# W1's load begun behind the filter's half swaps, the last group's evacuations reordered on ScalarE and VectorE, and 12 identity matmuls where 28 were

## The chip, the cores and the metric

The kernel runs on one core of a Trainium2 chip. The metric is the device time of one execution in microseconds (us). On one core a run is called slow if it lies over 1.5% above the fastest of its kernel. Each run also carries the mean clock that TensorE was granted, 1.000 being full speed.

Engines in the profile: PE is TensorE (PEld its weight loads), DVE is VectorE, ACT is ScalarE, POOL is GpSimd, SP is SyncE, whose sequencer (SPq) issues nearly all DMAs here.

## The reference, cut to what matters

```python
x = A_q                                              # 2048 tokens x 512 channels, bf16
x = x + A(layernorm(x), A_k, A_v, A_shift_k, A_ssm_k, A_ssm_D)
x = x + B(layernorm(x), B_w1, B_b1, B_w2, B_b2)
# both once more
# A(q, ...): kv = shift(k) * v;  y = irfft(rfft(kv) * rfft(ssm_k)) + kv * ssm_D;  q * y
# B(x, ...): gelu(layernorm(x) @ w1 + b1) @ w2 + b2
```

`y` in A depends on `k`, `v` and the filter only, so the kernel computes the long convolution once. It is a two-stage transform by matrices: filter (K), input (U), product (T), and back (V, Y). Then come eight MLP groups (four token groups, twice), of two matmul stages each, which need W1 and W2.

## The kernel before

The program is a list of named pieces, and one string fixes the order on every engine. The letter behind the dot is the engine (P, D, A, G, S for PE, DVE, ACT, POOL and SP); digits are buffer slots. Each engine works through its pieces strictly in this order, waiting where data is missing (DVE waits 1.48 us for a swap ahead of T00, for instance, with its later pieces behind it).

```python
ORDER = """ ...
... lM.S ... sw10.S ... U0T0.P0 pb0.G
w1.S K215e.A ... sw01.S ... sw00.S kv2.P12 ... U2T0.S1 ... U1T0.S2 ... U1T1.S ... U2T1.S ... sw11.S X11e.A0 ...
U3T0.S0 ... U3T1.S ... X30.P0 ... V32f.A gs0.D V33f.A TP22.S Y02e.A TP03.P3
V33r.A ga1.D TP03e.A TP31.S gs1.D V32r.A Y03.P1 TP30.S Y03e.A TP13.P0 gl0.D TP23.P3 TP13e.A TP33.P2 lx1.S TP23e.A
Y10.P0 gl1.D gp0.G ... gb0.D gp1.G gb1.D LT0.P0 TP33e.D LT1.P1 LT0e.A gb2.D TP21.S LT1e.A
m10x0.P3 pa10.D m10x1.P2 ge0x0.A pa11.D LT2.P0 lx2.S m10y0.P1 w2.S LT2e.D ge0x1.A pb1.G ...
"""
# w1: W1, 1.4 MB, one load from HBM
w1 = load("w1", W1t[:], B_w1.rearrange("(ct p) f -> p ct f", p=P), 3600)
# sw00 .. sw11: the filter's spectrum with its halves swapped, SBUF to SBUF, 1 MB each
def swap(it, off=off):
    for a in range(2):
        queue(it).dma_start(at(KSW + off, [[1, 16 * 256]], a, 64, 2), at(off, [[1, 16 * 256]], 1 - a, 64, 2))
# U1T0 .. U3T1: DMA transposes that feed the second transform stage X10 .. X33
nc.sync.dma_start_transpose(ztv(xown or it, [NA, P])[:, 16 * h:16 * h + 16, :],
                            ztv(own, [NA * P])[:, 2048 * h:2048 * h + 2048])
# T00 ..: DVE multiplies a spectrum by the filter and by the swapped filter (L528)
eng.tensor_tensor(spec(), x2, spec(), ALU.mult)
# ... cut ...
IDLE = (28, 0, 0)
for t in range(IDLE[h]):                              # L683, ahead of LT0's transposes
    nc.tensor.matmul(o.bitcast(F32)[:, 0, 0:64], IDt[:], IDt[:, 0:64], start=True, stop=True)
```

Names used below: T00 is the first spectral multiply, needing swap `sw00`. U3T0 and U3T1 are the last pair of transposes, X30 is the matmul group that needs U3T0. TP03 and TP13 are PE transposes of the output side, with TP03e the evacuation of the first. Y03 needs TP03e. V32r and V33r are the remainders of two evacuations, which TP13 needs. LT2e evacuates PE transposes that end late. pa11 is the second half of group 1's layer norm statistics. m110 is the first full gelu block of group 1.

Of the kernel before, what the change touches and what calls it, by code (L numbers as in the profile page):

```python
# [20 lines left out]
K200.P1 K2T0e.D K206.P2 K200e.A lk2.S K3T1.P3 K206e.D kv0.P01 K3T1e.A lk1.S K207.P2 kvm01.D K2T1.P3 K207e.A kvm00.D  # L21
K2T1e.A K3T0.P2 lM.S U0S0.P0 K3T0e.D U0S1.P1 U0S0e.A4 K204.P3 U0S1e.D K210.P2 K204e.A K211.P0 K210e.A K211e.D K212.P1
K213.P3 K212e.A U0S3.P2 K213e.D U0S2.P0 U0S3e.A K205.P1 U0S2e.D sw10.S K216.P3 K215.P2 K216e.A K205e.D U0T0.P0 pb0.G
w1.S K215e.A K202.P3 U0T0e.D5 sw01.S K203.P1 K202e.A K201.P2 K203e.D X00.P0 K201e.A U0T1.P3 X00e.A0 sw00.S kv2.P12
U0T1e.D kv1.P03 kvm20.D kvm21.D kvm11.D U2S0.P1 U2S1.P2 U2S0e.A6 kvm10.D U2S1e.A U2S2.P1 U2S2e.D U2S3.P0 U1S0.P3
U2S3e.A U1S3.P2 U1S0e.D0 U1S1.P1 U1S3e.A U2T0.S1 U1S2.P0 U1S1e.D K217.P3 U1S2e.A X01.P2 T00.D K217e.A K214.P1 U1T0.S2
X03.P0 K214e.A X02.P3 X01e.D1 X02e.A2 V00.P1 T01.D X03e.A0 kv3.P23 U1T1.S T02.D V00e.A3 T03.D X20.P0 pc00.G U2T1.S
V01.P1 kvm31.D X20e.A1 V01e.A kvm30.D X10.P0 X10e.A2 X11.P1 T20.D pc01.G U3S0.P2 sw11.S X11e.A0 U3S3.P3 T10.D X13.P0
U3S0e.A4 U3S2.P1 X13e.D1 U3S2e.A V10.P2 U3S3e.A T11.D X12.P0 X21.P1 V10e.A5 V03.P3 X12e.D2 X21e.A0 U3S1.P2 T13.D
V02.P0 U3S1e.A V20.P1 T12.D V03e.A U3T0.S0 V13.P2 V20e.D6 V02e.A V12.P3 V13e.A T21.D U3T1.S X23.P0 V12e.A X22.P1  # L30
X23e.D1 V11.P2 X22e.A2 V21.P3 TP00.S2 T23.D V11e.A X30.P0 V21e.A X31.P1 T22.D V23.P2 X31e.A0 V22.P3 V23e.D TP01.S
X30e.A1 X32.P1 T31.D V22e.A X33.P2 TP10.S1 Y00.P0 X33e.A2 T30.D V31.P3 X32e.A0 TP02.S T33.D Y01.P2 Y00e.A V30.P1
Y01e.A TP12.S T32.D V33.P0 V30e.A4 ga0.D V32.P2 TP11.S V31e.A Y02.P1 ho.G V32f.A gs0.D V33f.A TP22.S Y02e.A TP03.P3
V33r.A ga1.D TP03e.A TP31.S gs1.D V32r.A Y03.P1 TP30.S Y03e.A TP13.P0 gl0.D TP23.P3 TP13e.A TP33.P2 lx1.S TP23e.A
Y10.P0 gl1.D gp0.G TP20.S Y10e.A Y11.P3 Y11e.A gb0.D gp1.G gb1.D LT0.P0 TP33e.D LT1.P1 LT0e.A gb2.D TP21.S LT1e.A
m10x0.P3 pa10.D m10x1.P2 ge0x0.A pa11.D LT2.P0 lx2.S m10y0.P1 w2.S LT2e.D ge0x1.A pb1.G m10y1.P3 ge0y0.A TP32.S
m10z0.P0 pc10.D pc11.D ge0y1.A pd10.D m10z1.P2 ge0z0.A pd11.D m10z2.P1 ge0z1.A pe10.D Y21.P3 lx3.S ge0z2.A Y20.P0
pe11.D Y20e.A m200.P2 Y21e.A pa21.D pf1.G pg11.A pa20.D pg10.A lt11.S m201.P1 pa30.D pb2.G lt10.S pc20.A ad00.D pa31.D
pc21.A pa40.D m110.P0 pb3.G pc31.A pd21.D m111.P3 pd20.D ge10.A m112.P2 ge11.A pe21.D m113.P0 ge12.A pe20.D m114.P3
# [70 lines left out]
class _Plan:  # L110
# [7 lines left out]
    def add(self, name, cost, deps, fn, take=(), free=(), after=(), dma=0, tr=0):  # L118
        it = dict(name=name, cost=cost, deps=[d for d in deps if d is not None], fn=fn, take=list(take), slot={},
                  free=list(free), after=list(after), dma=dma, tr=tr)  # L120
        self.items.append(it)
        return it
# [15 lines left out]
def kernel(ctx: ExitStack, tc: tile.TileContext, A_q, A_k, A_v, A_shift_k, A_ssm_k, A_ssm_D,  # L138
# [186 lines left out]
    def load(name, dst, src, ns, deps=(), after=()):  # L325
        return add(name, {"S": 400, **QUEUE.get(name, {})}, deps, lambda it: queue(it).dma_start(dst, src), dma=ns, after=after)
# [227 lines left out]
    w1 = load("w1", W1t[:], B_w1.rearrange("(ct p) f -> p ct f", p=P), 3600)  # L554
# [5 lines left out]
    w2 = add("w2", {"S": 1300}, Vall[:8], w2load, dma=3900)  # L560
# [93 lines left out]
    POOLED = ("pc00", "pc01")  # L654
    CH = ((0, 1), (1, 2), (2, 4))
    GLC = ((0, 2), (2, 4))
    IDLE = (28, 0, 0)

    def gate_first(ln):
        gs = []  # L660
# [16 lines left out]
        for h, (a, b) in enumerate(CH):  # L677
# [3 lines left out]
            def mms(o, h=h, a=a, b=b):  # L681
                for t in range(IDLE[h]):
                    nc.tensor.matmul(o.bitcast(F32)[:, 0, 0:64], IDt[:], IDt[:, 0:64], start=True, stop=True)  # L683
                for i in range(a, b):
                    for ct in range(CT):
                        nc.tensor.transpose(o[:, CT * (i - a) + ct, :], lna0[:, i, ct * P:(ct + 1) * P], IDt[:])
# [124 lines left out]
```

## Time and profile before

| | before |
|---|---|
| time, six runs | 250.77 us median (249.75 to 253.33) |
| profiled run | span 249.2 us, mean clock 0.992 |
| T00's wait on the swap | 1.48 us |
| U3T0: issued, needed by X30 | 66.49, 71.53 us |
| 28 identity matmuls | 0.98 us |
| m110 starts | 111.12 us, without a wait |

Page of the kernel before, its strips of 40 slices of 6.2 us each (busy tenths; the granted clock in tenths; the DMA engines' busy tenths).

```profile
PE   7999999877999689999999999999999999999994
PEclk9999999999999799999999999999999999999999
DMA  6999999999399899440401240400310250030132
```

PE is full from slice 16 on, which is the MLP. What comes earlier decides when that stretch begins. The one 7 of the clock strip is a short stretch at half speed.

Waits view of the kernel before (engine, output, line, who ended the wait; us in total, times, longest), then its timeline (start us, duration us, engine, line, operation; in brackets the idle time ahead and who ended it).

```profile
DVE low L528 <- DMA low<-low: 1.5, 1, 1.5
```

```profile
48.72 1.21 DVE L359 CAST ZT_77<-p_89 128x1024 bf16<-128x1024 f32 x1
51.41 1.23 DVE L528 TENSOR_TENSOR low<-xb_84,low 128x2048 bf16<-128x2048 bf16 x1 [1.48 <-DMA low<-low]
...
66.49 4.44 SPq L477 DMA_TRANSPOSE ZT_77<-ZT_81  x2
71.53 0.61 PE L517 MATMUL p_88<-ZT_77,Wt 128*128 128x128 bf16 x8
...
81.23 0.62 PE L583 MATMUL p_91<-IDt,ZT_81 128*128 128x128 bf16 x8 [0.41 <-ACT ZT_81 L544]
83.33 0.41 PE L597 MATMUL p_89<-ZT_79,GPt 128*64 128x512 bf16 x2 [1.49 <-ACT ZT_79 L335]
84.04 0.62 PE L583 MATMUL p_88<-IDt,ZT_81 128*128 128x128 bf16 x8 [0.30 <-ACT ZT_81 L544]
88.47 0.98 PE L683 MATMUL p_88<-IDt 128*128 128x64 bf16 x28 [0.32 <-ACT high L335]
...
111.12 1.89 PE L738 MATMUL p_88<-low,W1t 128*128 128x512 bf16 x8
```

DVE starts T00 1.48 us late, for a swap still on its way. Further down, X30 (71.53 us) begins with no wait shown, 5.0 us after U3T0 was issued. TP03 (81.23) and TP13 (84.04) start 2.81 us apart. Windows view (stretch; length, busy time of PE, PEld, DVE, ACT and POOL with counts, granted clock, DMA share, GB/s):

```profile
44.00:46.00 2.00, 1.30 (x11) 1.02 (x12) 2.00 (x2) 1.33 (x2) 0.47 (x1) 1.00 1.02 411
46.00:48.00 2.00, 2.00 (x19) 1.57 (x17) 1.78 (x3) 1.69 (x3) 0.00 (x0) 1.00 1.02 427
...
64.00:66.00 2.00, 2.00 (x35) 1.91 (x33) 2.00 (x3) 1.92 (x3) 0.00 (x0) 1.00 0.00 0
...
84.00:88.00 4.00, 3.96 (x32) 2.59 (x32) 3.29 (x15) 3.02 (x4) 0.73 (x2) 0.57 0.93 200
```

DMA is full at 44 to 48 us, when the swaps are awaited, and empty at 64 to 66 us. The clock of 0.57 over 84 to 88 us is the half-speed stretch, some 3.4 us of it (us by us from 84: 0.77, 0.50, 0.50, 0.52, then 1.00).

### The profile page before, as it was taken

The page shows a single profiled execution, that of the slowest core. Times are in us where ns is not written, and L with a number is a line of the kernel's source. Part 1 is how long each engine was busy: PE and PEld are TensorE (multiplying, and loading weights), DVE is VectorE, ACT ScalarE, POOL GpSimd, SP SyncE. Part 2 cuts the span into 40 slices and gives each one's busy share as a digit, 9 for nine tenths or more (in the row PEclk, how much of TensorE's full clock was granted, in tenths as well). Part 3 has the DMA queues.
Part 4 walks back from the last instruction along what each step waited for, and adds up shares of the span by engine and source line. Part 5 has one row for each costly group of instructions (what it writes and reads, how often), then busy time and mean ns, then how long its engine had stood idle before and what let it go on. Part 6 is the DMA issues. An engine that isn't in the chain of part 4 may idle for free.

```text
span 249.2 us, 4803 instructions
## 1 busy us (share of the span) xinstructions
PE 234.9 (94%) x1910; PEld 146.5 (59%) x1919; DVE 170.4 (68%) x337; ACT 150.0 (60%) x217; POOL 50.6 (20%) x78
## 2 busy tenths in 40 slices
PE   7999999877999689999999999999999999999994
PEld 7888879676997579444444444444444444444443
DVE  2778697979999898999899967459749210110322
ACT  2598894778999869977738296172065463064000
POOL 4189970105001111230401121010110100000000
PEclk9999999999999799999999999999999999999999
DMA  6999999999399899440401240400310250030132
GB/s 228 269 420 161 241 393 293 360 184 235 115 189 187 171 224 256 108 84 1 86 3 37 49 84 3 84 0 1 72 15 0 45 123 3 0 84 0 45 73 54
DMA packets 55306, 31.02 MB, mean 125 GB/s; under 512 B 49810, under 2 KB 51956, under 8 KB 54260
## 3 DMA queue, kind: packets, MB, share of 16 engines
q1 hardware_dynamic: 54130, 30.38, 52.0%
q10 hardware_dynamic: 1074, 0.33, 0.6%
q8 instruction: 15, 0.25, 0.4%
q0 software_dynamic: 80, 0.00, 0.2%
q14 instruction: 7, 0.06, 0.1%
HBM read 12.36 MB, written 2.10 MB: 58 GB/s over the span
## 4 chain that ended last, share of the span: by engine, by line
PE 74%; DMA 9%; DVE 7%; ACT 6%; issue 2%; SPq 0%; DVEq 0%
PE p_90 L764 9%; PE p_91 L764 9%; PE p_88 L738 8%; PE p_89 L764 8%; PE p_91 L738 8%; PE p_90 L738 8%; PE p_89 L738 6%; DMA high<-in_A_k_dram 6%; PE p_88 L764 5%; DMA low<-in_A_ssm_k_dram 3%; ACT low L335 2%; ACT ZT_81 L544 1%; PE p_91 L536 1%; DVE low L528 1%; DVE high L469 1%
## 5 line engine op out<-in xcount | busy, mean ns | idle before, releaser
L738 PEld LDWEIGHTS <-W1t 128*128 128x128 bf16 (+1 forms) x440 | 40.2, 100 | 36.8 <-issue 0.6
L764 PEld LDWEIGHTS <-low 128*128 128x128 bf16 (+1 forms) x363 | 35.3, 98 | 41.2 <-issue 0.8
L749 ACT ACTIVATE low<-p_91,B_72 128x512 bf16<-128x512 f32 (+2 forms) x31 | 15.7, 581 | 17.1 <-PE p_90 L764 6.4
L749 ACT ACTIVATE low<-p_90,B_72 128x512 bf16<-128x512 f32 (+4 forms) x27 | 15.3, 633 | 17.5 <-PE p_89 L764 10.3
L749 ACT ACTIVATE low<-p_88,B_72 128x512 bf16<-128x512 f32 (+2 forms) x26 | 15.6, 658 | 14.0 <-PE p_89 L764 9.8
L764 PE MATMUL p_90<-low 128*128 128x512 bf16 (+3 forms) x107 | 23.4, 368 | 0.2
L738 PE MATMUL p_88<-low,W1t 128*128 128x512 bf16 (+2 forms) x104 | 22.9, 362 | 0.0
L764 PE MATMUL p_91<-low 128*128 128x512 bf16 (+1 forms) x95 | 22.0, 379 | 0.2
L738 PE MATMUL p_91<-low,W1t 128*128 128x512 bf16 (+2 forms) x124 | 21.7, 322 | 0.5 <-ACT low L335 0.5
L772 DVE TENSOR_TENSOR high<-p_91,high 128x1024 bf16<-128x1024 f32 (+1 forms) x5 | 5.6, 1115 | 24.1 <-PE p_91 L764 24.1
L738 PE MATMUL p_90<-low,W1t 128*128 128x512 bf16 (+4 forms) x108 | 21.8, 345 | 0.0
L764 PE MATMUL p_89<-low 128*128 128x512 bf16 (+3 forms) x99 | 21.0, 367 | 0.0
L738 PE MATMUL p_89<-low,W1t 128*128 128x512 bf16 (+4 forms) x104 | 17.8, 317 | 0.0
L536 PEld LDWEIGHTS <-low 128*128 128x128 bf16 x256 | 14.7, 98 | 3.0 <-DVE low L528 2.7
L749 ACT ACTIVATE low<-p_89,B_72 128x512 bf16<-128x512 f32 (+4 forms) x26 | 13.1, 577 | 1.3 <-PE p_89 L738 1.3
L287 ACT ACTIVATE high<-high,lnm_99,lrs_98 128x512 bf16<-128x512 bf16 x12 | 9.0, 840 | 7.2 <-POOL lnm_99 L276 7.2
L616 DVE TENSOR_TENSOR high<-high 128x1024 bf16<-128x1024 bf16 (+1 forms) x16 | 10.7, 668 | 2.8 <-ACT high L287 1.9
L764 PE MATMUL p_88<-low 128*128 128x512 bf16 (+1 forms) x53 | 12.3, 379 | 0.1
L772 DVE TENSOR_TENSOR high<-p_89,high 128x1024 bf16<-128x1024 f32 (+1 forms) x4 | 4.1, 1025 | 9.3 <-PE p_89 L764 9.3
L264 DVE BATCH_NORM_STATS2 lst_104<-high 128x6 f32<-128x512 bf16 x16 | 10.3, 683 | 0.3 <-DMA high<-in_A_q_dram 0.2
L264 DVE BATCH_NORM_STATS2 lst_96<-high 128x6 f32<-128x512 bf16 x16 | 10.2, 682 | 0.1
L274 POOL TENSOR_TENSOR lrs_98<-lrs_98,mhalf 128x4 f32<-128x4 f32 x4 | 4.0, 1007 | 30.4 <-DVE lnm_99 L271 30.4
(220 smaller groups left out, 442.8 us busy)
## 6 DMA issues: line engine op xcount, KB each, us to landing
low<-low SPq DMA_DIRECT2D x8, 512.0 KB, 11.0
low<-in_A_ssm_k_dram SPq DMA_DIRECT2D x4, 512.0 KB, 6.1
high<-in_A_v_dram SPq DMA_DIRECT2D x2, 1024.0 KB
high<-tabM SPq DMA_DIRECT2D x1, 2048.0 KB, 9.7
high<-in_A_q_dram SPq DMA_DIRECT2D x6, 256.0 KB, 5.4
W1t<-in_B_w_dram SPq DMA_DIRECT2D x1, 1376.0 KB, 10.7
low<-in_B_w_dram SPq DMA_DIRECT2D x1, 1280.0 KB, 8.8
Wt<-tabW SPq DMA_DIRECT2D x1, 1024.0 KB, 14.3
```

The costliest lines, as they stand in the source:

```text
L264: nc.vector.bn_stats(self.st[:, i, h, :], xg(g, i, i + 1, c0, c9)[:, 0, :])
L274: nc.gpsimd.tensor_tensor(self.rs[:, a:b], self.rs[:, a:b], mhalf[:, a:b], ALU.pow)
L287: nc.scalar.activation(dst[:, i, :], xs, AF.Identity, bias=bi, scale=sc)
L335: nc.scalar.activation(d, s, AF.Copy)
L469: nc.vector.tensor_tensor(us, k, us, ALU.mult)
L528: eng.tensor_tensor(spec(), x2, spec(), ALU.mult)
L536: nc.tensor.matmul(o[:, i, :], T[:, r, i, :], Mt[:, k0 + i, r, :], start=r == 0, stop=r == 1)
L616: nc.vector.tensor_tensor(tmp[:, a:b, c0:c9], ln[:, a:b, c0:c9], ys, ALU.mult)
L738: nc.tensor.matmul(o[0:m, ft - fts[0], :], W1t[:, ct, ft * P:ft * P + m], lnT[n % 3][:, a:b, ct, :], start=ct == 0, stop=ct == CT - 1)
L749: nc.scalar.activation(hT[n % 2][0:m, ft, a * P:b * P], psv(pe, dims)[0:m, ft - fts[0], :], AF.Gelu_apprx_tanh, bias=B1[0:m, ft:ft + 1])
L764: nc.tensor.matmul(o[:, i - a, 0:c9 - c0], hT[n % 2][0:m, ft, i * P:(i + 1) * P], W2t[0:m, ft, c0:c9], start=ft == 0, stop=ft == FT - 1)
L772: nc.vector.tensor_tensor(xs, psv(pe, [2, D])[:, 0:b - a, 0:c9 - c0], xs, ALU.add)
```

## The change

Its intent: keep W1's transfer out of the way of the swaps that T00 awaits; let Y03 start sooner by evacuating TP03 first; bring LT2's evacuation and gb2 forward on DVE; spend fewer identity matmuls. The diff, with unmoved words cut:

```diff
-w1.S K215e.A ... sw01.S ... sw00.S ... U2T0.S1 ... U1T0.S2 ... U1T1.S ... U2T1.S ... sw11.S X11e.A0
+K215e.A ... sw01.S ... sw00.S ... U2T0.S1 ... U1T0.S2 ... U1T1.S ... U2T1.S ... sw11.S w1.S X11e.A0
-TP03.P3 V33r.A ga1.D TP03e.A TP31.S gs1.D V32r.A Y03.P1
+TP03.P3 ga1.D TP03e.A V33r.A TP31.S gs1.D V32r.A Y03.P1
-LT0.P0 TP33e.D LT1.P1 LT0e.A gb2.D TP21.S LT1e.A
+LT0.P0 LT1.P1 LT0e.A gb2.D TP33e.D TP21.S LT1e.A
-m10x1.P2 ge0x0.A pa11.D LT2.P0 lx2.S m10y0.P1 w2.S LT2e.D ge0x1.A pb1.G
+m10x1.P2 ge0x0.A LT2.P0 lx2.S m10y0.P1 w2.S LT2e.D pa11.D ge0x1.A pb1.G
-    IDLE = (28, 0, 0)
+    IDLE = (12, 0, 0)
```

More of the change, by code (lines that the diff above doesn't have):

```diff
@@ L23 @@
 K213.P3 K212e.A U0S3.P2 K213e.D U0S2.P0 U0S3e.A K205.P1 U0S2e.D sw10.S K216.P3 K215.P2 K216e.A K205e.D U0T0.P0 pb0.G
-w1.S K215e.A K202.P3 U0T0e.D5 sw01.S K203.P1 K202e.A K201.P2 K203e.D X00.P0 K201e.A U0T1.P3 X00e.A0 sw00.S kv2.P12
-U0T1e.D kv1.P03 kvm20.D kvm21.D kvm11.D U2S0.P1 U2S1.P2 U2S0e.A6 kvm10.D U2S1e.A U2S2.P1 U2S2e.D U2S3.P0 U1S0.P3
-U2S3e.A U1S3.P2 U1S0e.D0 U1S1.P1 U1S3e.A U2T0.S1 U1S2.P0 U1S1e.D K217.P3 U1S2e.A X01.P2 T00.D K217e.A K214.P1 U1T0.S2
-X03.P0 K214e.A X02.P3 X01e.D1 X02e.A2 V00.P1 T01.D X03e.A0 kv3.P23 U1T1.S T02.D V00e.A3 T03.D X20.P0 pc00.G U2T1.S
-V01.P1 kvm31.D X20e.A1 V01e.A kvm30.D X10.P0 X10e.A2 X11.P1 T20.D pc01.G U3S0.P2 sw11.S X11e.A0 U3S3.P3 T10.D X13.P0
+K215e.A K202.P3 U0T0e.D5 sw01.S K203.P1 K202e.A K201.P2 K203e.D X00.P0 K201e.A U0T1.P3 X00e.A0 sw00.S kv2.P12 U0T1e.D
+kv1.P03 kvm20.D kvm21.D kvm11.D U2S0.P1 U2S1.P2 U2S0e.A6 kvm10.D U2S1e.A U2S2.P1 U2S2e.D U2S3.P0 U1S0.P3 U2S3e.A
+U1S3.P2 U1S0e.D0 U1S1.P1 U1S3e.A U2T0.S1 U1S2.P0 U1S1e.D K217.P3 U1S2e.A X01.P2 T00.D K217e.A K214.P1 U1T0.S2 X03.P0
+K214e.A X02.P3 X01e.D1 X02e.A2 V00.P1 T01.D X03e.A0 kv3.P23 U1T1.S T02.D V00e.A3 T03.D X20.P0 pc00.G U2T1.S V01.P1
+kvm31.D X20e.A1 V01e.A kvm30.D X10.P0 X10e.A2 X11.P1 T20.D pc01.G U3S0.P2 sw11.S w1.S X11e.A0 U3S3.P3 T10.D X13.P0
 U3S0e.A4 U3S2.P1 X13e.D1 U3S2e.A V10.P2 U3S3e.A T11.D X12.P0 X21.P1 V10e.A5 V03.P3 X12e.D2 X21e.A0 U3S1.P2 T13.D
@@ L33 @@
 Y01e.A TP12.S T32.D V33.P0 V30e.A4 ga0.D V32.P2 TP11.S V31e.A Y02.P1 ho.G V32f.A gs0.D V33f.A TP22.S Y02e.A TP03.P3
-V33r.A ga1.D TP03e.A TP31.S gs1.D V32r.A Y03.P1 TP30.S Y03e.A TP13.P0 gl0.D TP23.P3 TP13e.A TP33.P2 lx1.S TP23e.A
-Y10.P0 gl1.D gp0.G TP20.S Y10e.A Y11.P3 Y11e.A gb0.D gp1.G gb1.D LT0.P0 TP33e.D LT1.P1 LT0e.A gb2.D TP21.S LT1e.A
-m10x0.P3 pa10.D m10x1.P2 ge0x0.A pa11.D LT2.P0 lx2.S m10y0.P1 w2.S LT2e.D ge0x1.A pb1.G m10y1.P3 ge0y0.A TP32.S
+ga1.D TP03e.A V33r.A TP31.S gs1.D V32r.A Y03.P1 TP30.S Y03e.A TP13.P0 gl0.D TP23.P3 TP13e.A TP33.P2 lx1.S TP23e.A
+Y10.P0 gl1.D gp0.G TP20.S Y10e.A Y11.P3 Y11e.A gb0.D gp1.G gb1.D LT0.P0 LT1.P1 LT0e.A gb2.D TP33e.D TP21.S LT1e.A
+m10x0.P3 pa10.D m10x1.P2 ge0x0.A LT2.P0 lx2.S m10y0.P1 w2.S LT2e.D pa11.D ge0x1.A pb1.G m10y1.P3 ge0y0.A TP32.S
 m10z0.P0 pc10.D pc11.D ge0y1.A pd10.D m10z1.P2 ge0z0.A pd11.D m10z2.P1 ge0z1.A pe10.D Y21.P3 lx3.S ge0z2.A Y20.P0
```

## The prediction

> **What bounds the kernel.** From about 102 us to the end it is TensorE: in the windows view PE is busy 140.6 of 141.0 us from 104 to 245 us, with 1.73 us per eight-matmul block and no waits. The change touches nothing there. So it can only move the moment at which that stretch starts, set by the first 102 us. Before: DVE is busy nearly without a gap from 51.4 to 79.3 us (27 pieces, about 1.13 us apart, in the DVE timeline), then the last filter group passes ACT and PE (79 to 90 us).
>
> **Step 1, W1's load.** Its 1.4 MB are issued at 35.8 us, ahead of three of the half swaps. The DMA queues are full there (share about 1.0, 300 to 430 GB/s). The waits view shows one DVE wait on these swaps: 1.48 us before the first spectral multiply, 49.93 to 51.41 us. At about 330 GB/s W1 is worth some 4 us of DMA time (estimate), so the swap then lands before 49.9 us and the wait goes: -1.5 us. DVE is full behind it, so this carries to 79 us. The skew-in transposes behind (2.8 to 3.4 us each to issue) should be quicker too. W1 now goes out at 56 to 60 us, into an empty hole (64 to 66 us: 0 GB/s), and is needed only at 88 us. It may hold up the last pair of transposes (issued at 66.5 us, needed at 71.5): +0.3 us expected. [...]
>
> **Step 2, ScalarE.** The transpose's evacuation (0.92 us) now stands ahead of a remainder evacuation (0.70 us) that used to fill the 0.36 us in which its transpose finishes. Y03 starts about 0.7 us sooner, but its evacuation and the next transposes (which wait for both remainders) come 0.36 us later; the gate waits for that evacuation (84.47 to 84.51 us). Expected +0.3 us. PE ran at clock 0.50 from 84.4 to 87.9 us, after idling 1.49 us. [...] The idle time is shared out otherwise, not removed, so I expect this cold stretch still, or moved.
>
> **Step 3, identity matmuls.** 28 take 0.98 us on the chain, at 88.47 us, when their input's producer (DVE) is already done at 88.5. 16 fewer: -0.56 us.
>
> **Step 4, VectorE.** The second statistics of group 1 now stand behind the evacuation of LT2, whose transposes end only at 93.4 us. DVE idles about 1.2 us there, and group 1's gate starts some 2.2 us later than the shift allows. Before, its last transposed load was issued about 106.8 us, landing 3.2 us later at 110.0; its consumer on PE came at 111.28, so slack was about 1.3 us. Now PE would be there at 109.6 and the load at about 110.8: a new PE wait of about 1.2 us eats most of the gain.
>
> **Sum.** -1.5 +0.3 +0.3 -0.6 +1.2 = -0.3; if the last is smaller than I think, -1.7. I predict 249.9 us, between 248.4 and 251.3; faster over 2% 0.02, same 0.96, slower 0.02.
>
> **What would show it.** No DVE wait on the swap DMA; PE at the first full gelu block (111.28 us before) between 109.5 and 111.3, with a wait there on the transposed load; 12 identity matmuls taking 0.4 us; ACT idle about 0.4 us ahead of the moved evacuation; W1 landing before 72 us.
>
> **What would make it wrong.** The half clock vanishing (-1 us) or falling on the first gelu blocks (+1.7 us); W1 delaying the last transposes; slack at group 1 other than read.

That PE's idling brings the half-speed stretch was the estimate from this one trace, where the stretch follows 1.49 us of idle time. The clock's -1 and +1.7 us under what would make it wrong are estimates too: 1.7 is half of the stretch measured here (3.4 to 3.5 us); for -1 the record gives no source, and the runs counted below differ by 0.95 us between none and one stretch.

## The result

| | before | changed |
|---|---|---|
| median of all runs | 250.72 us (40 runs) | 254.82 us (20 runs, 253.12 to 257.61) |
| fast runs, ratio | | 1.0155, 95% interval 1.0132 to 1.0178 |
| profiled run | span 249.2 us, clock 0.992 | span 251.8 us, clock 0.993 |

A ratio is the mean time of one kernel's fast runs over that of the other's of the same rounds, so it is not quite the ratio of the medians. The change is slower by 1.55%, about 3.9 us, where 249.9 us was predicted, with 251.3 us as the upper end. It stays within 2%, the class that was given 0.96, but with the opposite sign: a small gain was forecast and a clear loss measured. That the class fits is due to its width, not to the account behind it.

Waits view of the changed kernel:

```profile
PE p_88 L517 <- DMA ZT_77<-ZT_81: 2.3, 1, 2.3
PE p_88 L738 <- DMA low<-high: 1.9, 1, 1.9
```

Its timeline:

```profile
49.73 1.21 DVE L528 TENSOR_TENSOR low<-xb_84,low 128x2048 bf16<-128x2048 bf16 x1
...
60.06 0.73 SPq L326 DMA_DIRECT2D W1t<-in_B_w_dram  x1
64.79 6.93 SPq L477 DMA_TRANSPOSE ZT_77<-ZT_81  x2
...
72.30 0.62 PE L517 MATMUL p_88<-ZT_77,Wt 128*128 128x128 bf16 x8 [2.30 <-DMA ZT_77<-ZT_81]
...
82.00 0.62 PE L583 MATMUL p_91<-IDt,ZT_81 128*128 128x128 bf16 x8 [0.41 <-ACT ZT_81 L544]
83.73 0.41 PE L597 MATMUL p_89<-ZT_79,GPt 128*64 128x512 bf16 x2 [1.11 <-ACT ZT_79 L335]
85.14 1.03 PE L583 MATMUL p_88<-IDt,ZT_81 128*128 128x128 bf16 x8 [1.00 <-ACT ZT_81 L544]
89.55 0.51 PE L683 MATMUL p_88<-IDt 128*128 128x64 bf16 x12 [0.69 <-ACT high L335]
...
113.77 0.59 PE L738 MATMUL p_88<-low,W1t 128*128 128x512 bf16 x2 [1.87 <-DMA low<-high]
```

Its windows:

```profile
44.00:46.00 2.00, 1.32 (x12) 1.04 (x12) 2.00 (x2) 1.46 (x2) 0.34 (x1) 1.00 0.07 29
46.00:48.00 2.00, 2.00 (x18) 1.57 (x17) 1.78 (x3) 1.69 (x3) 0.00 (x0) 1.00 0.00 0
...
64.00:66.00 2.00, 2.00 (x40) 2.00 (x38) 2.00 (x3) 2.00 (x3) 0.00 (x0) 1.00 1.01 380
...
72.00:74.00 2.00, 1.70 (x31) 1.71 (x32) 0.00 (x0) 0.55 (x1) 0.00 (x0) 1.00 1.27 285
```

And from the chain of waits that ended last, the two DMA pieces (start, length):

```profile
64.79 7.46 DMA ZT_77<-ZT_81
...
109.51 4.12 DMA low<-high
```

T00 now starts at 49.73 us instead of 51.41, as foretold. PE arrives at X30 at 70.00 us (72.30 less its wait), 1.53 us ahead of the kernel before, and then waits 2.30 us: U3T0, issued at 64.79 us while W1 keeps the DMA engines at 380 GB/s, takes 7.46 us to land. So X30 starts 0.77 us later than before (72.30 against 71.53), although PE was there 1.53 us sooner. The hole in the DMA traffic has moved from 64 us, where U3T0 was issued into it, to 44 us, where nothing uses it. TP03 and TP13 are 3.14 us apart instead of 2.81. At m110 PE waits another 1.87 us.

The two profiled runs have the same clock and differ by 2.6 us, the medians by 4.1. The clocks of the 21 runs of the change (the profiled one and 20 more, among them one slow run) explain most of the rest. One stretch of 3.4 us at half speed (3.42 us in both profiled runs, by windows of 1 us from 84 us on) lowers the mean clock of a 250 us run by 3.4 x 0.5 / 250 = 0.0068. Counted this way (the deficit of the mean clock over 0.0068, rounded), with the 44 runs of the kernel before that were taken alongside the experiments, so not in the same rounds:

| half-speed stretches in a run | before: runs, mean us | changed: runs, mean us |
|---|---|---|
| 0 | 24, 250.07 | 1, 253.35 |
| 1 | 20, 251.02 | 8, 253.58 |
| 2 | | 7, 255.10 |
| 3 or 4 | | 5, 256.36 |

With one stretch on both sides the change costs 253.58 - 251.02 = 2.56 us. The kernel before has 20/44 = 0.45 stretches a run, the changed one (8 + 14 + 12 + 4)/21 = 1.8. An estimate from these means: the mean of the changed kernel's 20 fast runs lies 1.0 us above its runs with one stretch, that of the kernel before 0.5 us below its own, so the additional stretches cost about 1.5 us. With the 2.56 us that makes 4.1, against 3.9 by the ratio and 4.1 by the medians.

### The profile page after: what moved, and what is told of

The parts are those of the page before. It is cut to its first block, busy times and chain, and to the rows that moved or that the text cites. A ratio compares the mean times of both kernels' runs of the same rounds, so it can differ in the third digit from the quotient of the medians.

```text
span 251.8 us, 4773 instructions
## 1 busy us (share of the span) xinstructions
PE 234.3 (93%) x1894; PEld 146.2 (58%) x1903; DVE 170.1 (68%) x337; ACT 149.8 (59%) x217; POOL 50.1 (20%) x78
## 4 chain that ended last, share of the span: by engine, by line
PE 61%; DMA 14%; DVE 12%; ACT 6%; issue 4%; POOL 1%; SPq 0%; DVEq 0%
PE p_91 L764 8%; PE p_91 L738 8%; PE p_88 L738 8%; PE p_90 L738 7%; PE p_90 L764 7%; PE p_89 L764 6%; DMA high<-in_A_k_dram 6%; PE p_89 L738 5%; PE p_88 L764 5%; DMA ZT_77<-ZT_81 3%; DMA low<-in_A_ssm_k_dram 3%; DVE low L528 2%; DMA low<-high 2%; ACT ZT_81 L544 2%; DVE high L469 1%
```

## The experiments

All were run in five rounds beside the kernel before, on the same chip within a group (e1 to e4, e5 to e8, e9 to e12, e13 and e14), and all gave correct results. In their profiles line numbers are one or two off, as the order string was wrapped anew, and buffer numbers are missing. The reading in us is the ratio less 1, times the 250.3 to 250.8 us of the kernel before in that group.

### e1 to e4: each part of the change alone

The theory was that W1's new place and VectorE's reorder make the loss; the rival, that W1's move is the gain predicted and all the loss lies in the reorders.

```diff
 e1: ORDER  - pb0.G w1.S K215e.A        + sw11.S w1.S X11e.A0
 e2: ORDER  - V33r.A ga1.D TP03e.A      + ga1.D TP03e.A V33r.A
 e3: ORDER  - TP33e.D ... gb2.D         + gb2.D TP33e.D
            - pa11.D ... LT2e.D         + LT2e.D pa11.D
 e4: IDLE   - (28, 0, 0)                + (12, 0, 0)
```

Expected of e1: 

> Only the move of W1's load, from ahead of three half swaps to behind the last one. Theory (W1's transfer sits in the DMA queues ahead of the last pair of transposes, and so gives back more than the swaps gain): DVE's 1.48 us wait on the swap is gone, PE waits some 2 to 2.5 us for the last pair of transposes near 72 us, net +0.8 to +1.5 us. Rival (the move of W1 is a gain of about 1 us, as predicted, and the loss lies in the reorders): -1 us.

Expected of e2: 

> Only ScalarE's reorder (the transpose's evacuation ahead of the first remainder). Theory: the next transposes wait for both remainders, so they and the gate come 0.3 to 0.4 us later: +0.3 to +0.6 us. Rival (the sooner Y03 helps the clock, or the chain): 0 to -0.5 us.

Expected of e3: 

> Only VectorE's two reorders. Theory: the second statistics of group 1 wait behind the evacuation of LT2, so group 1's transposed tile lands some 2 us later and PE waits at its first full gelu block: +1.2 to +2.2 us. Rival (there is slack enough): 0, and no such wait.

Expected of e4: 

> Only 12 identity matmuls in place of 28. Theory A: they are plain work on the chain: -0.4 to -0.6 us, and the granted clock of the runs is as before. Theory B: the 28 keep PE's clock up, and with 12 more runs fall to half clock for one more stretch of 3.4 us: +0.3 to +1.5 us, with clocks of 0.987 and lower in more of the runs.

(Theory B of e4 is a guess that no earlier run had shown; its 3.4 us is the stretch of the kernel before, 84.5 to 88 us.)

| | median us | ratio to before | 95% interval | us |
|---|---|---|---|---|
| e1, W1 alone | 251.77 | 1.0074 | 1.0043 to 1.0106 | +1.85 |
| e2, ScalarE alone | 250.61 | 1.0011 | 0.9979 to 1.0042 | +0.3 |
| e3, VectorE alone | 251.77 | 1.0059 | 1.0029 to 1.0089 | +1.5 |
| e4, 12 identity matmuls | 250.10 | 0.9994 | 0.9955 to 1.0033 | -0.15 |
| sum | | | | +3.5 |
| whole change | 254.82 | 1.0155 | 1.0132 to 1.0178 | +3.9 |

The parts nearly add up, and two of them make the loss. The rival about W1 falls: its move alone costs 1.85 us. That is more than the theory's upper end of 1.5; it brings half-speed stretches too, 1.3 a run by the count above against 0.45 before, and e13 below tests that. The timeline of e3 shows VectorE's part, here beside that of the kernel before. First before:

```profile
91.62 1.28 DVE L264 BATCH_NORM_STATS2 lst_104<-high 128x6 f32<-128x512 bf16 x2
...
93.52 0.69 DVE L337 COPY low<-p_88 128x1024 bf16<-128x1024 bf16 x1
94.73 1.38 DVE L289 TENSOR_SCALAR high<-high,lrs_106,lnm_107 128x512 bf16<-128x512 bf16 x4 [0.51 <-POOL lnm_107 L276]
```

Then e3:

```profile
92.69 0.69 DVE L336 COPY low<-p 128x1024 bf16<-128x1024 bf16 x1 [0.49 <-PE p L685]
93.29 1.28 DVE L263 BATCH_NORM_STATS2 lst<-high 128x6 f32<-128x512 bf16 x2
96.39 0.73 DVE L288 TENSOR_SCALAR high<-high,lrs,lnm 128x512 bf16<-128x512 bf16 x2 [1.33 <-POOL lnm L275]
...
111.32 2.97 PE L737 MATMUL p<-low,W1t 128*128 128x512 bf16 x13 [0.87 <-DMA low<-high]
```

Before, pa11 (91.62 us) filled the time until LT2's transposes were done, so the copy at 93.52 us hardly waited. In e3 DVE waits for PE first and does pa11 afterwards. The next step, which needs POOL's scale made from pa11, starts 1.66 us later (96.39 against 94.73) although PE runs ahead, and at m110 PE waits 0.87 us. Its time, +1.5 us, is more than this wait; the profiled run had no half-speed stretch, and what makes up the rest was not looked into.

The time of e2 is inconclusive: its interval holds both theories. Its trace is not. TP03 and TP13 are 3.15 us apart (80.99 and 84.14 us), against 2.81 before and 3.14 in the change. The reorder costs 0.34 us at this place, as predicted. e4's time is inconclusive as well; its 12 identity matmuls and those of the change save 0.47 us of PE time (0.51 against 0.98), and no clear gain can be told from that.

### e5, e6, e7: the same load elsewhere

```diff
 e5: ORDER  - pb0.G w1.S K215e.A        + sw00.S w1.S kv2.P12
 e6: ORDER  - pb0.G w1.S K215e.A        + U3T1.S w1.S X23.P0
 e7: ORDER  - pb0.G w1.S K215e.A        + sw11.S w1.G X11e.A0
```

Expected of e5: 

> Only the move of W1's load, but to just behind the third half swap, some 20 us sooner than in the change. Theory (what hurts is W1's 1.4 MB lying in the queues ahead of the last pair of transposes): W1 fills the hole that the changed kernel's trace shows from 44 to 48 us (0 to 29 GB/s), the DVE wait on the swap is gone, the last pair of transposes lands about 5 us after issue, PE does not wait for it: -0.8 to -1.6 us. Rival (moving W1 behind the swaps costs wherever it goes, as it delays other transposes): 0 to +1 us, with PE waits on the earlier pairs.

Expected of e6: 

> Only the move of W1's load, to behind the last pair of skew-in transposes (about 68 us). Theory: the pair lands about 5 us after issue again, so the wait near 72 us is gone, but W1 now lies ahead of the transposes of the output side, of which the first is needed by PE some 5 us later: PE waits there instead, 1 to 3 us; net 0 to +2 us. Rival (only the last pair was tight): -1 to -1.5 us.

Expected of e7: 

> W1's load moved as in the change, but issued by GpSimd[...]. Theory A (the transposes stand behind W1 in one queue, in order): beside another queue they get a share at once and land in 5 to 6 us, PE waits under 1 us: -1 to 0 us. Theory B (the bytes alone count, whichever queue they are in): the transposes take 7 us and more as in the change, PE waits about 2.3 us: +0.8 to +1.9 us.

| | ratio | 95% interval | us | U3T0's time on the queue | PE's new wait |
|---|---|---|---|---|---|
| before | 1 | | | 1.83 us | none |
| e5, behind the third swap | 0.9980 | 0.9948 to 1.0012 | -0.5 | 1.88 us | 1.22 us at X10, 1.17 us at X30 |
| e1, behind the last swap | 1.0074 | 1.0043 to 1.0106 | +1.85 | 4.05 us | 2.39 us at X30 |
| e6, behind the last pair | 1.0160 | 1.0122 to 1.0198 | +4.0 | 1.92 us | 3.27 us at Y00 |
| e7, as e1, issued by POOL | 1.0147 | 1.0114 to 1.0180 | +3.7 | 4.96 us | 3.33 us at X30 |

(The time on the queue is how long SP's sequencer is busy with issuing that one transpose.) T00 starts at 49.5 to 49.8 us in all four variants: every place behind the third swap frees DVE from the wait. What differs is which transposes follow W1. In e6 the pair is quick again and the next consumer, PE's Y00, waits instead. That loss is twice what was expected at most. Part of the losses of e6 and e7 is clock: they had 1.8 and 2.2 half-speed stretches a run. e6's profiled run, with one, took 252.52 us and its other five, with two, 254.5 to 255.2. e7 refutes the idea that the transposes only stand behind W1 in one ordered queue:

```profile
57.53 0.87 POOL L325 DMA_DIRECT2D W1t<-in_B_w_dram  x1
...
64.63 4.96 SPq L476 DMA_TRANSPOSE ZT<-ZT  x1
...
73.17 1.89 PE L516 MATMUL p<-ZT,Wt 128*128 128x128 bf16 x16 [3.33 <-DMA ZT<-ZT]
```

These lines are e7's timeline. W1 is issued by another engine, 2.6 us earlier than in e1, and takes 12.2 us to land instead of 8.8; the transposes get no better service beside it than behind it: U3T0 takes 4.96 us on SP's queue and 8.5 us to land, against 4.05 and 7.55 us in e1. So a load that another engine issued holds the transpose up as well. It fits theory B in direction, though the wait was 1 us above what B expected and the time, +3.7 us, twice its upper end. e7 is not the same load on another queue and nothing else: it went out ahead of sw11 (58.14 us), not behind it, and the profile page of e7 shows its 1.4 MB on q0, "software_dynamic", where e1 has them on q1, "hardware_dynamic". Which of these made the load itself slower was not tried.

e5's time is inconclusive: -0.5 us is less than the theory asked for, and the interval holds 0. Its trace shows that the rival is partly right:

```profile
57.44 1.07 PE L516 MATMUL p<-ZT,Wt 128*128 128x128 bf16 x16 [1.22 <-DMA ZT<-ZT]
...
71.79 1.07 PE L516 MATMUL p<-ZT,Wt 128*128 128x128 bf16 x16 [1.17 <-DMA ZT<-ZT]
```

W1 now lies ahead of the earlier pair of transposes, and PE waits 1.22 us at X10 (57.44 us). That delays the evacuations which U3T0 needs, so U3T0 is issued at 65.56 us, where e1 has 64.73. Its profiled run also shows 1.17 us of wait at X30, with no W1 left in the queues (it had landed 9.1 us after its issue at 40.7 us). In e11, with the same place for W1, X10 waited likewise (1.34 us), but X30 did not. So the landing of the last pair varies by about 1 us between runs (U3T0: 6.18 us in e5, 4.9 us at most in e11, where X30 starts at 70.36 us after an issue at 65.46), for a reason that stays open.

### e8: which of VectorE's two reorders

```diff
 e8: ORDER  - pa11.D ... LT2e.D         + LT2e.D pa11.D
```

Expected of e8: 

> Of VectorE's two reorders only the second: the second statistics of group 1 behind the evacuation of LT2. Theory (this one makes the loss): DVE idles 0.5 to 1.3 us before that evacuation, PE waits about 0.9 us for group 1's transposed tile: +0.9 to +1.6 us. Rival (the other reorder makes it, or both together): under +0.5 us.

Measured: 251.44 us, ratio 1.0038 (1.0008 to 1.0068), +0.95 us; DVE idles 1.8 us ahead of LT2's evacuation and PE waits 0.9 us at m110, as in e3. The idle time is above the 1.3 us expected at most, the time as expected. So this reorder alone loses, though only just clear of noise. The intervals of e3 and e8 overlap, so whether the other reorder adds anything is not settled.

### e9: half the load

```diff
+    w1r = B_w1.rearrange("(ct p) f -> p ct f", p=P)
-    w1 = load("w1", W1t[:], B_w1.rearrange("(ct p) f -> p ct f", p=P), 3600)
+    w1 = load("w1", W1t[:, 0:2, :], w1r[:, 0:2, :], 1800)
+    w1b = load("w1b", W1t[:, 2:4, :], w1r[:, 2:4, :], 1800)
 ORDER  - pb0.G w1.S K215e.A      + sw00.S w1.S      + sw11.S w1b.S
```

Expected of e9: 

> W1's load in two halves of 0.7 MB: one behind the third half swap, one where the change has the whole. So far: the last pair's first transpose took 7.5 us from issue to landing with all of W1 ahead of it, 6.2 us with none, and PE waited 2.3 and 1.2 us. Theory (the bytes ahead of it count): about 6.8 us, PE waits 1.5 to 2.0 us, time between the two: +0.3 to +1.2 us over the kernel before. Rival (a plain load of any size ahead costs the same, as a matter of order): 7.5 us and 2.3 us, +1.5 us.

Measured: 250.05 us, ratio 0.9971 (0.9942 to 0.9999), -0.7 us. This missed both expectations: PE had no wait at X30 and 0.23 us at X32. U3T0's time on the queue was 2.91 us, between the 1.9 us of no W1 and the 4.0 us of the whole. So the bytes count for the time on the queue. Half of them, issued at 59.92 us, were further through when U3T0 was issued at 64.64 us: the window of 64 to 66 us has 246 GB/s, against 398 in e1. That what is still in flight then decides, and not the bytes issued ahead, is a reading of these two windows and was not tested by itself. For PE's wait half a load can't be told from none: it was 0 here and 1.37 us in e14 with half, 1.17 us in e5 and 0 in e11 with none.

### e10, e12, e13: the change with one thing put back, and the clock

```diff
 e10: the change, IDLE  - (12, 0, 0)  + (28, 0, 0)
 e12: the change, ORDER - LT2e.D pa11.D  + pa11.D ... LT2e.D
 e13: the change, and ahead of X30's matmuls (shortened: the program picks X30 by a parameter):
+    for t in range(64):
+        nc.tensor.matmul(o[:, 0, 0:64], IDt[:], IDt[:, 0:64], start=True, stop=True)
```

Expected of e10: 

> The whole change, but with the 28 identity matmuls kept. Theory A (they are plain work): 0.4 to 0.6 us slower than the change, so +4.2 to +4.7 us over the kernel before, clocks spread as in the change (most at 0.987 and below). Theory B (the missing 16 cost clock): the same as the change or faster, +3 to +4 us, with more runs at 0.993 and 1.0.

Expected of e12: 

> The change with only the statistics of group 1 put back ahead of the evacuation of LT2. Theory (the parts add up): 1.0 to 1.9 us faster than the change, so +2.0 to +2.9 us over the kernel before; no PE wait at the first full gelu block. Rival (the late W1 delays this stage anyway): +3.5 us, wait still there.

Expected of e13: 

> The whole change, with 64 identity matmuls set in PE's 2.3 us wait for the last pair of transposes (about 35 ns each, so about 2.2 us, done before the transposes land). Theory (the idle PE there starts an extra stretch of half clock in most runs): with PE busy there, runs show 0.993 or 1.0 and about one stretch less on average; 0.8 to 1.5 us faster than the change, so +2.4 to +3.2 us over the kernel before. Rival (the stretches fall at random, or come from other waits): as the change, +3.7 to +4.3 us, clocks of 0.987 and lower in half of the runs.

| | ratio | 95% interval | us | half-speed stretches a run |
|---|---|---|---|---|
| whole change (measured with its own 20 runs) | 1.0155 | 1.0132 to 1.0178 | +3.9 | 1.8 |
| e10, 28 identity matmuls kept | 1.0147 | 1.0113 to 1.0181 | +3.7 | 1.7 |
| e12, statistics put back | 1.0083 | 1.0039 to 1.0127 | +2.1 | 1.8 |
| e13, PE kept busy at X30 | 1.0112 | 1.0086 to 1.0139 | +2.8 | 0.7 |

e12 confirms VectorE's part from the other side: the wait at m110 is gone, and 1.8 us come back. Its timeline at m110:

```profile
112.12 3.19 PE L737 MATMUL p<-low,W1t 128*128 128x512 bf16 x14
```

e10 is inconclusive: neither theory about the identity matmuls can be told from it. But with e4 it shows that they decide little. e13 supports the clock's part. The windows of e1, where PE waits for U3T0 as in the change:

```profile
70.00:72.00 2.00, 0.00 (x0) 0.00 (x0) 1.53 (x2) 1.12 (x2) 0.00 (x0) 1.00 1.17 102
72.00:74.00 2.00, 1.67 (x27) 1.68 (x28) 0.00 (x0) 0.52 (x1) 0.00 (x0) 0.90 1.27 286
74.00:76.00 2.00, 2.00 (x22) 2.00 (x20) 1.10 (x1) 1.42 (x2) 0.00 (x0) 0.50 0.99 193
76.00:78.00 2.00, 2.00 (x24) 1.67 (x23) 2.00 (x3) 1.28 (x2) 0.00 (x0) 0.74 0.56 102
```

And of e13:

```profile
70.00:72.00 2.00, 1.73 (x60) 1.64 (x57) 1.46 (x2) 1.04 (x2) 0.00 (x0) 1.00 1.17 101
72.00:74.00 2.00, 1.72 (x31) 1.72 (x31) 0.00 (x0) 0.58 (x1) 0.00 (x0) 1.00 1.27 285
74.00:76.00 2.00, 1.96 (x37) 1.83 (x33) 1.67 (x2) 2.00 (x3) 0.00 (x0) 1.00 1.67 100
76.00:78.00 2.00, 1.28 (x19) 0.88 (x17) 2.00 (x3) 2.00 (x3) 0.00 (x0) 1.00 0.83 182
```

In e1 PE idles 2.39 us, and shortly after it resumes the clock is at 0.50 for 0.4 + 2.0 + 1.0 = 3.4 us (0.90 in the second window is 0.4 us at half speed, 0.74 in the fourth is 1.0 us). In e13 PE still gets X30 at 72.28 us, but it was busy with 64 idle multiplies meanwhile, and the clock stays at 1.00 from 70 to 78 us. By mean clock its six runs count as none or one stretch each, and it is about 1.1 us faster than the change (1.55% less 1.12% of 250.7 us; the two intervals overlap slightly). Not every such wait starts a stretch. Of the five profiled runs in which PE waited over 2.2 us at X30, e1 and e10 went to half speed within 1.5 us of its end (0.90 and 0.69 over 72 to 74 us), e7 about 1 us ahead of its end (0.58 over 72 to 73 us); e12 (2.51 us, its clock 1.00 from 70 to 78 us) and the changed kernel itself (2.30 us, its clock 1.00 from 70 to 80 us) did not. So e13 shows the cost over many runs, and no trace of the changed kernel shows such a stretch at X30. The stretch measures 3.4 us in e1, e10, e13, the kernel before and the changed one (in the last three at 84 to 89 us), and 6.8 us in e7, twice that. Why some runs have it at X30 and others don't was not shown.

### e11 and e14: the change repaired

e11 keeps the parts that were not shown to lose: W1 behind the third swap, 12 identity matmuls, gb2 ahead of TP33e. ScalarE's order and pa11 are as before. e14 is e11 with W1 in two halves as in e9.

```diff
 e11: ORDER  - pb0.G w1.S K215e.A       + sw00.S w1.S kv2.P12
             - TP33e.D ... gb2.D        + gb2.D TP33e.D
      IDLE   - (28, 0, 0)               + (12, 0, 0)
 e14: e11, and w1 split, the second half behind sw11.S
```

Expected of e11: 

> The change without its two bad parts: W1 behind the third half swap, the evacuation of LT2 and ScalarE's order as before, 12 identity matmuls and the harmless VectorE reorder kept. Theory: the swap's wait is gone, no late PE wait at the first full gelu block: -0.6 to -1.2 us, faster than both kernels. Rival (the gain at the swaps is always given back at the last pair of transposes, and the identity matmuls are worth nothing): 0.

Expected of e14: 

> The repaired change of e11 with W1's load in two halves, the first behind the third half swap, the second behind the last one. If the gains of e9 (-0.7 us, split alone) and e11 (-1.3 us) partly add: -1.4 to -1.8 us. If both take the same gain at the swaps: as e11, -1.0 to -1.4 us.

e11: 249.13 us, ratio 0.9947 (0.9915 to 0.9979), -1.3 us: faster than the kernel before, clear of noise though far from 2%, and faster than the change. Its timeline:

```profile
49.55 1.21 DVE L527 TENSOR_TENSOR low<-xb,low 128x2048 bf16<-128x2048 bf16 x1
...
70.36 1.06 PE L516 MATMUL p<-ZT,Wt 128*128 128x128 bf16 x16
...
109.28 4.48 PE L737 MATMUL p<-low,W1t 128*128 128x512 bf16 x20
```

T00 and X30 start without a wait, the price being the 1.34 us at X10 (X30 at 70.36 us, against 71.53 before), and m110 comes at 109.28 us, also without a wait, against 111.12. e14: 250.06 us, ratio 0.9988 (0.9960 to 1.0015), -0.3 us. That is worse than either expectation; its profiled run shows PE waiting 1.37 us for the last pair, where e9, with the same two halves, showed none at X30. Whether half of W1 at the later place is on the edge, or this is the variation that e5 and e11 show with no load there, stays open. e11 has the better reading and is the only version of the two that is faster than the kernel before clear of noise, but their intervals overlap, and so do those of e5 (-0.5 us) and e9 (-0.7 us) with both: that e11 beats these is not shown.

## Why the prediction was wrong

- What bounds the kernel: right. The span less the start of m110 is 138.0 to 138.3 us in the kernel before, the change, e1, e3, e11 and e12 alike, so each loss lies ahead of it.
- Step 1, the wait on the swap: right. It is gone; T00 starts 1.68 us earlier.
- Step 1, "It may hold up the last pair of transposes (issued at 66.5 us, needed at 71.5): +0.3 us expected": this is the step that failed. The mechanism was named, the size was off by 2 us: 2.30 us of PE wait. The hole at 64 us was taken for free room, but U3T0 is issued into it, and landed within 5.0 us. With W1 in flight it took 7.46 us, and 7.40 to 7.67 in e1, e10 and e12 (in e5, with no load in flight, 6.18). And with PE arriving 1.53 us sooner, the transpose was needed sooner too: the gain itself used up the slack. e1 shows the net, clock included, +1.85 us where -1.2 us was summed.
- Step 2, ScalarE: right in the trace (+0.33 us between TP03 and TP13 against +0.3 predicted; Y03 came 0.37 us sooner after TP03, not 0.7); its time alone, +0.3 us, is inside the noise.
- Step 3, identity matmuls: 0.47 us of PE time saved, where 0.56 was predicted; not resolved in the time (-0.15 us, interval of about 1 us to either side).
- Step 4, VectorE: right in kind. PE waits for group 1's transposed tile at m110. The wait was sized as 1.2 us and "eats most of the gain"; it measured 1.87 us in the change, 0.87 us in e3, and there was no gain to eat. e12 gets 1.8 us back by undoing it.
- The clock: listed among what could make it wrong, at 0 in the sum. The wait at X30 starts additional half-speed stretches in some of the runs. e13, whose edit only fills that idle time, has 0.7 stretches a run against 1.8 and is about 1.1 us faster than the change.

The failed sum was -1.5 +0.3 +0.3 -0.6 +1.2. At equal clock the runs put in its place: -1.5 for the swap (PE's lead at X30), +2.3 for the last pair, +0.3 ScalarE, -0.5 identity matmuls, +1.9 at m110, together +2.5, which the two profiles (2.6 us apart) agree with. The rest, 1.3 to 1.6 us by the ratio or the medians, is put down to the clock: e13 measures 1.1 us of it at X30, the remainder is an estimate from the count of stretches.

## What to carry to other kernels

A hole in the DMA traffic is not free room: ask which small transfer is issued into it, how soon its consumer needs it, and whether the change itself makes that consumer arrive sooner. (Here U3T0, issued behind 2 us of 0 GB/s, landed within 5.0 us; issued into 380 GB/s it took 7.46 us, and PE came 1.53 us sooner.) Move a load into a hole only where it has drained before the next urgent transfer is issued; here the hole that the move left behind, 20 us earlier, was the better one in e11's trace (no wait at X30), at the price of a shorter wait elsewhere (1.34 us at X10). On an engine that works in order, a piece that waits for another engine should stay behind the pieces that are ready (putting pa11 back ahead of LT2e brought 1.8 us in e12), and a new idle gap on TensorE can cost twice, once as the wait (2.30 us at X30) and, in some of the runs, once as clock (about 1.1 us on the mean, by e13).

## Idle gaps and the clock, transposes beside a load: the figures in one place

- The length of an idle gap on PE does not settle whether half clock follows. It followed gaps of 2.39 us in e1 and 2.24 us in e10, came inside a gap of 3.33 us in e7, and in the kernel before followed gaps of 1.49 and 0.30 us in the 3 us ahead of it. But it did not follow 2.30 us in the change, 2.51 us in e12, or 1.11 and 1.00 us in e2. One more stretch in a run went with about 1 us of time in the kernel before and 1.5 us in the change.
- How a plain load in flight holds up a DMA transpose: the same transpose, U3T0, kept the issuing queue for 1.83 to 1.92 us with no load in flight, 2.91 and 2.95 with half of one, 3.98 to 4.15 with 1.4 MB, and 4.96 with the 1.4 MB issued by POOL. From issue to landing it took 7.40 to 7.67 us with the load ahead of it (8.5 in e7), 6.53 in e14 with half of it (X30's start less 0.05 us), against 5.0 us at most before and 6.18 us in e5 with none.
